# Linear attention and a gated feed-forward block: six tokens of r to a row, 384-token steps, a 32x32 convolution and a new order

## The chip, the cores and the metric

The kernel runs on one core of a Trainium2 chip. The metric is the device time of one execution in microseconds (us), as the median of several runs. A core has a tensor engine (PE, with its weight loads shown apart as PEld), a vector engine (DVE), a scalar engine (ACT), GpSimd (POOL) and a sync engine (SP), each with its own in-order queue of instructions, and 16 DMA engines that all queues share. PE writes to PSUM[...]; DVE and ACT read it.

## The reference

Two blocks in a row. The first is linear attention with a decaying state, for 4 batches, 8 heads, 768 tokens and 48 channels a head:

```python
for t in range(S):
    kt, vt, rt = k[:, :, t], v[:, :, t], r[:, :, t]
    cur = np.einsum('bhd,bhe->bhde', u[None] * kt, vt)
    y[:, :, t] = np.einsum('bhd,bhde->bhe', rt, state + cur)
    state = w[None, :, :, None] * state + np.einsum('bhd,bhe->bhde', kt, vt)
```

The second takes y, with the heads side by side, as x of 384 channels. It has a causal convolution of five taps for each channel, a sigmoid of it as a gate, and two 384x384 products:

```python
for j in range(5):
    gate_pre += conv_w[j] * xp[:, j:j + S, :]       # xp: x with four zero tokens ahead
out = (sigmoid(gate_pre) * (x @ w_val)) @ w_out
```

All inputs and the output are float32.

## The kernel before

**Tiling.** The tokens of a batch are cut into chunks of 128 (`C`), and two chunks make a unit (`W` = 256 tokens). Each batch has three units, so there are 12 units, numbered 0 to 11. The loop over time becomes, inside a chunk, a masked product of r and k (`attn`, `mask_at`) and, across chunks, a state that is carried (`state`, `carry`, `decay`). The powers of w are put into r and k beforehand by tables of exponentials (`dr`, `dk`, made by `decay_r` and `decay_k`).

**Loads.** `load_kv` (L69) brings one chunk of k or v with tokens on the partitions, so that each row is one token of one head, 192 bytes. `load_r` (L76) brings a unit of r with two neighbouring tokens on a partition, 384 bytes to a row. The scaled r is transposed on PE in two sets of 128 tokens, and the eviction `evac_r` (L282) puts the two sets back in order by writing with a stride of two. The weights `w_val` and `w_out` come in one transfer each.

**One unit, in stages.** Each stage has a token in the order: RS scales r (L260) and KS scales k (L289), mostly on POOL; RT and KT transpose them on PE (L274, L312), RE and KE evict them on ACT (L282, L322). PR multiplies the transposed k by r on DVE (L331), S sums it into the bonus of each token (L343), SE evicts that (L355), and DV multiplies v by it on POOL (L358). CV casts v to bfloat16 on ACT (L298). A is the product of k and r (L372), M its mask on DVE (L385). KV adds a chunk to the state (L399), ID adds the old state on DVE (L411), ZE multiplies it by the decay (L416). YD and Y collect y in PSUM (L427, L441), YE casts it to x, transposed, on ACT (L470).

**Feed-forward block.** It also works on units of 256 tokens. C is the convolution (L485): the five taps are diagonal 64x64 weights, and the products run on 64x64 tiles of the array. The 384 channels are three groups of 128; the third group is split over the two halves of the unit, so a unit needs two PSUM banks of 384 columns and 40 products. SG is the sigmoid on ACT (L498), V the product with `w_val` (L505, L514), HT its product with the gate on DVE (L527), O the product with `w_out` (L537), OE the eviction on ACT (L549), st the store (L553). The two chunks of the last unit go through smaller stages of their own (L575 to L652).

**The order.** The function emits each engine's instructions in the order of a long list of tokens, `ORDER`, that was found by a search; nothing reorders it afterwards. `RS:3` is the scaling of r for unit 3, `M:3.1` a mask of it, `k:3.0` a load; a star gives the stage to the other engine or queue. Since every engine works through its own part of this list in turn, the place of a token decides what it waits behind. Loads and stores stand in it too, nearly all on SP's queue; in before, all stores come after the last load. Waits between engines are put in from the data that the stages share. PSUM banks are handed out in turn (`bank`, eight buffers), and a buffer is taken again when its last reader is done.

Of the kernel before, what the change touches and what calls it, by code (L numbers as in the profile page):

```python
# [16 lines left out]
def kernel(  # L17
# [12 lines left out]
    nc = tc.nc  # L30
# [16 lines left out]
    ldr = ctx.enter_context(tc.tile_pool(name="ldr", bufs=6))  # L47
# [3 lines left out]
    outp = ctx.enter_context(tc.tile_pool(name="outp", bufs=11))  # L51
# [11 lines left out]
    def load_kv(n, cl, nm, eng):  # L63
        b, cu = divmod(n, NU)
        src, d = (k, k_st) if nm == "k" else (v, v_st)
        if n not in d:
            d[n] = ld.tile([128, U, H, D], F32, name=f"{nm}_st")
        t0 = cu * W + cl * C
        eng.dma_start(out=d[n][:, cl], in_=src[b, :, t0 : t0 + C, :].transpose([1, 0, 2]))  # L69

# [35 lines left out]
    io_i32 = consts.tile([128, 1], mybir.dt.int32)  # L106
    nc.gpsimd.iota(io_i32, pattern=[[0, 1]], base=0, channel_multiplier=1)
    io_j = consts.tile([128, 2], mybir.dt.int32)
    nc.gpsimd.iota(io_j, pattern=[[1, 2]], base=0, channel_multiplier=2)
    mask = consts.tile([128, 128], BF16)  # L110
    make_upper_triangular(nc, mask, val=1.0, diag=False)

    io_f = consts.tile([128, 1], F32)
    nc.vector.tensor_copy(io_f, io_i32)
    sc_k = consts.tile([128, U], F32)
    for cl in range(U):
        nc.vector.tensor_scalar(
            sc_k[:, cl : cl + 1], io_f, scalar1=-1.0, scalar2=float(C - 1 - cl * C),
            op0=ALU.mult, op1=ALU.add,
        )  # L120
    sc_r = consts.tile([128, 2], F32)
    nc.vector.tensor_copy(sc_r, io_j)
    nc.vector.tensor_scalar_add(sc_r, sc_r, float(-C))
# [4 lines left out]
    dr = consts.tile([128, H, 2, D], F32)  # L128

# [18 lines left out]
    def decay_r(x):  # L148
        for j in range(2):
            nc.scalar.activation(  # L150
                out=dr[:, halves(x), j, :],
                in_=lnw_bc[:, halves(x)],
                func=AF.Exp,
                scale=sc_r[:, j : j + 1],
            )

# [43 lines left out]
    nc.gpsimd.memset(wcm, 0.0)  # L200
    bdm = consts.tile([128, NP, 2, D], F32)
    nc.gpsimd.memset(bdm, 0.0)
    for par in range(2):
        nc.gpsimd.memset(bdm[64 * par : 64 * par + 64, :, par, :], 1.0)
# [3 lines left out]
    wv_st = consts.tile([128, NT, DM], F32)  # L208
    wo_st = consts.tile([128, NT, DM], F32)

    wval = consts.tile([128, NT, 4, 128], BF16)
    wout = consts.tile([128, 4, DM], BF16)
    cw5b = consts.tile([KW, DM], BF16)
    cwT = consts.tile([128, NT, KW], F32)
    cwd = consts.tile([128, NT, KW, 64], BF16)
    id64 = consts.tile([128, 64], BF16)

    for q in range(2):
        rows = slice(64 * q, 64 * q + 64)
        nc.vector.tensor_copy(id64[rows], ident[rows, rows])  # L220
# [11 lines left out]
    def cw_evac():  # L232
        nc.vector.tensor_copy(cwT, st["cw_ps"][:, :, 0:KW])

    def cw_diag():
        nc.vector.tensor_tensor(
            out=cwd.rearrange("p t k x -> p (t k) x"),
            in0=id64[:, None, :].to_broadcast([128, NT * KW, 64]),
            in1=cwT.rearrange("p t k -> p (t k)")[:, :, None].to_broadcast([128, NT * KW, 64]),
            op=ALU.mult,  # L240
        )

    def cast_wval():
        wv = wv_st.rearrange("p k (t x) -> p k t x", x=128)
        nc.gpsimd.tensor_copy(wval[:, :, 0::2, :], wv[:, :, 0::2, :])
        nc.gpsimd.tensor_copy(wval[:, :, 1::2, 64:128], wv[:, :, 1:3, 0:64])
        nc.gpsimd.tensor_copy(wval[:, :, 1::2, 0:64], wv[:, :, 1:3, 64:128])

    def cast_wout(part):
        if part:  # L250
            nc.scalar.copy(out=wout[64:128, 1::2, :], in_=wo_st[0:64, 1:3, :])
            nc.scalar.copy(out=wout[0:64, 1::2, :], in_=wo_st[64:128, 1:3, :])
        else:
            nc.gpsimd.tensor_copy(wout[:, 0::2, :], wo_st[:, 0::2, :])

    def scale_r(n, eng, ps=(0, NP)):
        hs = slice(2 * ps[0], 2 * ps[1])
        eng.tensor_tensor(  # L260
            out=rs_t[n % 2][:, :, ps[0] : ps[1], :, 0:D].rearrange("p s n a d -> p (n a) s d"),
            in0=r_st[n][:, hs],
            in1=dr[:, hs],
# [3 lines left out]
    def transp_r(n, ps=(0, NP)):  # L267
        if ("rT", n) not in st:
            st["rT", n] = wk.tile([128, NP, W], BF16, name="rT", bufs=3)
# [11 lines left out]
    def evac_r(n, ps=(0, NP)):  # L281
        nc.scalar.copy(  # L282
            out=st["rT", n][:, ps[0] : ps[1], :].rearrange("x n (i s) -> x s n i", s=2),
            in_=st["r_tr", n, ps[0]],
        )
# [10 lines left out]
    def cast_v(n):  # L296
        vb = vb_t[n % 4]
        nc.scalar.copy(  # L298
# [20 lines left out]
    def evac_k(n, cl=None):  # L319
        for cls, tr in st["tr", n]:  # L320
            if cl is None or cl == cls[0]:
                nc.scalar.copy(  # L322
                    out=st["kT", n].rearrange("x n (c i) -> x c n i", c=U)[:, cls[0] : cls[1]],
                    in_=tr,
# [84 lines left out]
    def carry(n, cl):  # L409
        kv_ps = st["kv_ps", n, cl]  # L410
        nc.vector.tensor_tensor(out=kv_ps, in0=kv_ps, in1=st["zin", n, cl], op=ALU.add)  # L411
# [55 lines left out]
    def evac_y(n, cl):  # L467
        b, cu = divmod(n, NU)
        t0 = PAD + cu * W + cl * C
        nc.scalar.copy(out=xT_t[b % 2][:, :, t0 : t0 + C], in_=st["y_ps", n, cl])  # L470


    def conv(n):
        b, cu = divmod(n, NU)
        xT, t0 = xT_t[b % 2], cu * W
        g_ps = [bank([128, W + C]) for i in range(2)]
        for T0, t1, tn in ((0, 0, W), (2, 0, 0)):
            for t in range(KW):
                for q in range(2):
                    for i in range(2):  # L480
                        T = 2 if T0 else i
                        c0, n0, o0 = (i * C, C, W) if T0 else (t1, tn, t1)
                        rows = slice(64 * q, 64 * q + 64)
                        qo = (q + i) % 2
                        nc.tensor.matmul(  # L485
                            out=g_ps[i][64 * qo : 64 * qo + 64, o0 : o0 + n0],
                            lhsT=cwd[rows, T, t, :],
                            rhs=xT[rows, T, t0 + c0 + t : t0 + c0 + t + n0],
                            start=(t == 0 and T0 == 0 and t1 == 0),
                            stop=(t == KW - 1),  # L490
                            skip_group_check=True,
                        )
        st["g_ps", n] = g_ps

    def gate_at(n, i):
        if ("gate", n) not in st:
            st["gate", n] = ffn.tile([128, 2, W + C], BF16, name="gate")
        nc.scalar.activation(out=st["gate", n][:, i], in_=st["g_ps", n][i], func=AF.Sigmoid)  # L498

    def value(n, i):  # L500
        b, cu = divmod(n, NU)
        xT, t0 = xT_t[b % 2], PAD + cu * W
        v_ps = bank()[:, 0 : W + C]
        for kt in range(NT):
            nc.tensor.matmul(  # L505
                out=v_ps[:, 0:W],
                lhsT=wval[:, kt, i, :],
                rhs=xT[:, kt, t0 : t0 + W],
                start=(kt == 0),
                stop=(kt == NT - 1),  # L510
                skip_group_check=True,
            )
        for kt in range(NT):
            nc.tensor.matmul(  # L514
                out=v_ps[:, W : W + C],
                lhsT=wval[:, kt, 2 + i, :],
                rhs=xT[:, kt, t0 + i * C : t0 + i * C + C],
                start=False,
                stop=(kt == NT - 1),
                skip_group_check=True,  # L520
            )
        st["v_ps", n, i] = v_ps

    def gated(n, i):
        if ("hT", n) not in st:
            st["hT", n] = ffn.tile([128, 2, W + C], BF16, name="hT")
        nc.vector.tensor_tensor(  # L527
            out=st["hT", n][:, i], in0=st["v_ps", n, i], in1=st["gate", n][:, i], op=ALU.mult
        )

    def project(n, cl):
        hT = st["hT", n]
        o_ps = bank()[:, 0:DM]
        parts = [(0, cl * C, 0), (1, cl * C, 1)]
        parts.insert(1 + cl, (cl, W, 2 + cl))
        for j, (i, c0, k) in enumerate(parts):
            nc.tensor.matmul(  # L537
                out=o_ps,
                lhsT=hT[:, i, c0 : c0 + C],
                rhs=wout[:, k, :],  # L540
                start=(j == 0),
                stop=(j == 2),
            )
        st["o_ps", n, cl] = o_ps

    def evac_o(n, cl):
        if ("o", n) not in st:
            st["o", n] = outp.tile([128, U, DM], F32, name="o_sb")
        nc.scalar.copy(out=st["o", n][:, cl, :], in_=st["o_ps", n, cl])  # L549

    def store(n):
        b, cu = divmod(n, NU)
        nc.sync.dma_start(  # L553
            out=out[b, cu * W : cu * W + W, :].rearrange("(c p) n -> p c n", p=128),
            in_=st["o", n],
        )

    HC = C // 2  # L560
    WL = C + HC

    def conv_l(n, cl):
        b, cu = divmod(n, NU)
        xT, t0 = xT_t[b % 2], cu * W + cl * C
        g_ps = [bank()[:, 0:WL] for i in range(2)]
        for T0 in (0, 2):
            for t in range(KW):
                for q in range(2):
# [262 lines left out]
```

## Time and profile before

| What | Value |
|---|---|
| Median of 3 runs | 103.78 us (103.75 to 104.38) |
| The profiled execution's own time | 103.68 us |
| Its span (first to last instruction) | 101.9 us |
| Granted PE clock, mean | 0.983 |
| Busy: PE, DVE, ACT, POOL | 84.5, 73.5, 72.7, 66.1 us |
| DMA packets, bytes | 67,505, 20.37 MB |
| Last product on PE ends (chain of waits) | 96.96 us |
| First store issued on SP | 75.90 us |

The profile is one execution seen by the hardware profiler. Its page gives busy time by engine, the span in 40 slices with a digit for the tenth of each slice that an engine was busy, the DMA queues, and groups of instructions. A group's row has its source line, engine and operation, what it writes and reads, the count, the busy time with the mean duration in nanoseconds, and the idle time ahead of it with what ended that idle time. The chain of waits follows the execution back from its end: each row is a start, a duration, and the work that held the end back at that time. A row of the waits has who waited, for whom, the sum in us, the times and the longest. A busy PE is one with at least one product in flight; several may overlap. Where many products follow each other, the time from the first of a stage to the first of the next is what the stage costs, and it is less than the count times the duration of one.

### The profile page before, as it was taken

Reading aid. Unit: us, or ns where it says so; the run is one execution under the profiler, and the core shown is the slowest. Engines: PE = TensorE matmul, PEld = TensorE weight load, DVE = VectorE, ACT = ScalarE, POOL = GpSimd, SP = SyncE. Lnnn points to the kernel's source line nnn. Section 1 sums busy time; section 2 is a strip of 40 time slices with the busy share of each in tenths; the row PEclk is TensorE's granted clock in tenths of the full one; section 3 lists DMA queues with packets and bytes.
Section 4 is the critical chain, followed back from the end, with each engine's and each line's share of the span. In section 5 each row is a group of like instructions: output and inputs, shape, how many; then the busy total and the mean of one; then the engine's idle time right before and its main releaser. Section 6 shows DMA issues by size and latency. Waiting matters only on the chain.

```text
span 101.9 us, 4626 instructions
## 1 busy us (share of the span) xinstructions
PE 84.5 (83%) x2017; PEld 69.4 (68%) x2017; DVE 73.5 (72%) x145; ACT 72.7 (71%) x126; POOL 66.1 (65%) x67
## 2 busy tenths in 40 slices
PE   1413987998969799989999999988999999999900
PEld 1202766876858587978887887876888788778500
DVE  4057798999765685889989998489678898980500
ACT  5457574999294998887988939688979868538510
POOL 7928678969499884999775686798692571400000
PEclk9999999999999999999999999999999999999985
DMA  0999999999989998999999999798989894750660
GB/s 7 253 220 168 234 175 192 270 244 171 277 165 249 203 216 180 200 185 250 173 191 223 187 248 222 142 204 187 185 162 251 306 363 145 271 198 7 250 218 5
DMA packets 67505, 20.37 MB, mean 200 GB/s; under 512 B 63510, under 2 KB 67484, under 8 KB 67484
## 3 DMA queue, kind: packets, MB, share of 16 engines
q1 hardware_dynamic: 64428, 19.18, 85.0%
q10 hardware_dynamic: 3056, 0.89, 4.0%
q8 instruction: 16, 0.26, 1.1%
q14 instruction: 5, 0.04, 0.1%
HBM read 15.35 MB, written 4.72 MB: 197 GB/s over the span
## 4 chain that ended last, share of the span: by engine, by line
PE 28%; SPq 24%; DMA 18%; POOL 12%; ACT 8%; issue 5%; POOLq 0%
SPq L69 19%; DMA v_st<-in_v_dram 15%; POOL dv L358 7%; PE bank L537 6%; PE bank L485 5%; PE bank L441 4%; POOL ks L289 4%; SPq L76 4%; DMA r_st<-in_r_dram 3%; ACT xT L470 2%; PE bank L505 2%; PE bank L427 2%; ACT kT L322 2%; PE bank L399 1%; ACT rT L282 1%
## 5 line engine op out<-in xcount | busy, mean ns | idle before, releaser
L385 DVE TENSOR_TENSOR at<-bank,mask 128x512 bf16<-128x512 f32 x48 | 30.9, 681 | 3.4 <-PE bank L372 3.3
L260 POOL TENSOR_TENSOR rs<-r_st,dr 128x768 bf16<-128x768 f32 x11 | 20.0, 1821 | 7.5 <-DMA r_st<-in_r_dram 7.5
L289 POOL TENSOR_TENSOR ks<-k_st,dk 128x768 bf16<-128x768 f32 x10 | 18.2, 1822 | 8.1 <-DMA k_st<-in_k_dram 4.4
L358 POOL TENSOR_TENSOR dv<-v_st,s_sb 128x768 bf16<-128x768 f32 x12 | 17.7, 1476 | 4.4 <-DVE s_sb L355 2.9
L282 ACT COPY rT<-bank 128x1024 bf16<-128x1024 bf16 (+1 forms) x13 | 15.9, 1231 | 2.6 <-PE bank L274 2.6
L322 ACT COPY kT<-bank 128x1024 bf16<-128x1024 bf16 (+1 forms) x13 | 12.5, 959 | 4.7 <-DVE pr L331 1.7
L527 DVE TENSOR_TENSOR hT<-bank,gate 128x384 bf16<-128x384 f32 x22 | 11.8, 552 | 4.2 <-PE bank L514 2.5
L470 ACT CAST xT<-bank 128x384 bf16<-128x384 f32 x24 | 11.0, 493 | 3.5 <-PE bank L441 3.5
L537 PE MATMUL bank<-wout,hT 128*128 128x384 bf16 x66 | 13.4, 327 | 0.0
L298 ACT CAST vb<-v_st 128x768 bf16<-128x768 f32 x12 | 10.0, 836 | 4.1 <-DMA v_st<-in_v_dram 4.1
L485 PE MATMUL bank<-xT,cwd 64*64 64x128 bf16 (+1 forms) x440 | 11.5, 245 | 0.9 <-ACT xT L470 0.4
L498 ACT ACTIVATE gate<-bank 128x384 bf16<-128x384 f32 x22 | 10.0, 493 | 2.6 <-PE bank L485 2.4
L485 PEld LDWEIGHTS <-cwd 64*64 64x64 bf16 x440 | 9.9, 106 | 2.5 <-issue 1.5
L549 ACT COPY o_sb<-bank 128x384 f32<-128x384 f32 x22 | 10.7, 501 | 1.2 <-PE bank L537 1.2
L505 PE MATMUL bank<-xT,wval 128*128 128x256 bf16 x66 | 10.8, 273 | 0.1
L312 PE MATMUL bank<-ident,ks 128*128 128x128 bf16 x96 | 8.8, 242 | 1.8 <-DVE ks L289 1.8
L372 PE MATMUL bank<-rT,kT 48*128 48x128 bf16 x192 | 9.0, 232 | 1.0 <-ACT kT L322 0.7
L331 DVE TENSOR_TENSOR pr<-bank,rT 128x1024 bf16<-128x1024 bf16 (+1 forms) x13 | 8.4, 645 | 1.9 <-ACT kT L322 1.3
L274 PE MATMUL bank<-ident,rs 128*128 128x128 bf16 x96 | 8.6, 242 | 1.1 <-DVE rs L260 0.8
L441 PE MATMUL bank<-at,vb 128*32 128x128 bf16 x384 | 9.0, 219 | 0.0
L312 PEld LDWEIGHTS <-ks 128*128 128x128 bf16 x96 | 6.8, 109 | 2.5 <-POOL rs L260 2.0
L274 PEld LDWEIGHTS <-rs 128*128 128x128 bf16 x96 | 6.7, 109 | 1.9 <-issue 1.0
(80 smaller groups left out, 137.8 us busy)
## 6 DMA issues: line engine op xcount, KB each, us to landing
k_st<-in_k_dram SPq DMA_DIRECT2D x24, 192.0 KB, 5.5
v_st<-in_v_dram SPq DMA_DIRECT2D x24, 192.0 KB, 4.5
out_dram<-o_sb SPq DMA_DIRECT2D x11, 384.0 KB, 4.5
r_st<-in_r_dram SPq DMA_DIRECT2D x9, 384.0 KB, 5.6
r_st<-in_r_dram ACTq DMA_DIRECT2D x2, 384.0 KB, 5.1
wv_st<-in_moe_w_val_dram SPq DMA_DIRECT2D x1, 576.0 KB, 6.2
wo_st<-in_moe_w_out_dram SPq DMA_DIRECT2D x1, 576.0 KB, 6.0
r_st<-in_r_dram SPq DMA_DIRECT2D x2, 192.0 KB, 3.5
```

The costliest lines, as they stand in the source:

```text
L69: eng.dma_start(out=d[n][:, cl], in_=src[b, :, t0 : t0 + C, :].transpose([1, 0, 2]))
L260: eng.tensor_tensor(out=rs_t[n % 2][:, :, ps[0] : ps[1], :, 0:D].rearrange("p s n a d -> p (n a) s d"), in0=r_st[n][:, hs], in1=dr[:, hs], ...
L274: nc.tensor.transpose(tr[:, s, p, :], rs_t[n % 2][:, s, ps[0] + p].rearrange("p a x -> p (a x)"), ident,)
L282: nc.scalar.copy(out=st["rT", n][:, ps[0] : ps[1], :].rearrange("x n (i s) -> x s n i", s=2), in_=st["r_tr", n, ps[0]],)
L289: eng.tensor_tensor(out=ks_t[n % 3][:, cs, :, :, 0:D].rearrange("p c n a d -> p c (n a) d"), in0=k_st[n][:, cs], in1=dk[:, cs], op=ALU.mult,)
L312: nc.tensor.transpose(tr[:, c, p, :], ks[:, cls[0] + c, p].rearrange("p a x -> p (a x)"), ident,)
L322: nc.scalar.copy(out=st["kT", n].rearrange("x n (c i) -> x c n i", c=U)[:, cls[0] : cls[1]], in_=tr,)
L358: eng.tensor_tensor(out=dv_t[n % 2].rearrange("p c (h d) -> p (c h) d", d=D), in0=v_st[n].rearrange("p c h d -> p (c h) d"), in1=st["s", n ...
L385: nc.vector.tensor_tensor(out=st["at", n, cl][:, par], in0=st["at_ps", n, cl][par], in1=mask[:, None, :].to_broadcast([128, NP, 128]), op= ...
L441: nc.tensor.matmul(out=y_ps[32 * q : 32 * q + 32, T, :], lhsT=lt, rhs=rh, start=False, stop=last, skip_group_check=True,)
L485: nc.tensor.matmul(out=g_ps[i][64 * qo : 64 * qo + 64, o0 : o0 + n0], lhsT=cwd[rows, T, t, :], rhs=xT[rows, T, t0 + c0 + t : t0 + c0 + t + ...
L537: nc.tensor.matmul(out=o_ps, lhsT=hT[:, i, c0 : c0 + C], rhs=wout[:, k, :], start=(j == 0), stop=(j == 2),)
```

## The change

Seven things are done together.

1. **r.** Batch 0 keeps its loads by unit. For batches 1 to 3, `load_rb` brings four heads of a whole batch at a time with six neighbouring tokens on a partition, 1,152 bytes to a row. A table `drb` of six exponentials of 128x384 is added (`decay_rb`, on ACT). "Unit" q of such a batch is now the token set {6p + 2q, 6p + 2q + 1}; `evac_r` writes into a transposed tile of the whole batch with a stride of six, so attention of the batch can begin when all three sets are there.
2. **Feed-forward steps.** They are 384 tokens, two a batch, and 384, 256 and 128 for the last batch: nine steps. The special stages for the last unit go.
3. **Convolution.** The taps are diagonal 32x32 weights, and a step has 5 x 3 x 4 = 60 products on 32x32 tiles, three PSUM banks a step. The channels of each group come out turned by a multiple of 32; the columns of `w_val` and the rows of `w_out` are turned to fit, the latter by five loads in place of one.
4. **Stores.** An output row of a partition is three neighbouring tokens, 4,608 bytes. The last product therefore reads `hT` with a stride of three. The staging buffers of the two weights are now two of the six buffers of the output ring.
5. **State.** The old state is added on PE by a product with the identity instead of on DVE.
6. **Engines.** Some evictions may go to DVE, some casts of v and the cast of `w_out` to POOL: four KE, six YE and four OE go to DVE, two CV to POOL; two RS and one KS more go to DVE. Some set-up moves between POOL and DVE.
7. **Order.** The whole list is new, searched with at most one engine reading a PSUM bank at a time. It has four groups of dummy products (three of 512 columns each, `D`) and places the store of step 2 ahead of the last load.

The core of the diff, with the old list left out:

```diff
-    ldr = ctx.enter_context(tc.tile_pool(name="ldr", bufs=6))
+    ldr = ctx.enter_context(tc.tile_pool(name="ldr", bufs=3))
...
-    outp = ctx.enter_context(tc.tile_pool(name="outp", bufs=11))
+    outp = ctx.enter_context(tc.tile_pool(name="outp", bufs=6))
...
+    G = 2 * NU
+
+    def load_rb(b, eng, x):
+        if ("rb", b) not in r_st:
+            r_st["rb", b] = ldr.tile([128, H, G, D], F32, name="rb_st", bufs=2)
+        hs = slice(H // 2 * x, H // 2 * x + H // 2)
+        eng.dma_start(
+            out=r_st["rb", b][:, hs].rearrange("p h s d -> p h (s d)"),
+            in_=r[b, hs].rearrange("h (p s) d -> p h (s d)", s=G),
+        )
...
+    def decay_rb(j):
+        nc.scalar.activation(out=drb[:, :, j, :], in_=lnw_bc, func=AF.Exp, scale=sg[:, j : j + 1])
...
+    wv_st = outp.tile([128, NT, DM], F32, name="o_sb")
+    wo_st = outp.tile([128, NT, DM], F32, name="o_sb")
+
+    wval = consts.tile([128, NT, NT, 128], BF16)
+    wout = consts.tile([128, NT, DM], BF16)
...
+    def load_wout(i):
+        T, (c0, f0, n0) = [(T, x) for T in range(NT) for x in turned(T)][i]
+        nc.sync.dma_start(
+            out=wo_st[c0 : c0 + n0, T, :], in_=moe_w_out[128 * T + f0 : 128 * T + f0 + n0, :]
+        )
+
+    def cast_wout(pool):
+        if pool:
+            nc.gpsimd.tensor_copy(wout, wo_st)
         else:
-            nc.gpsimd.tensor_copy(wout[:, 0::2, :], wo_st[:, 0::2, :])
-
-
+            nc.scalar.copy(out=wout, in_=wo_st)
...
+            in0=r_st["rb", b][:, hs, two] if b else r_st[n][:, hs],
+            in1=drb[:, hs, two] if b else dr[:, hs],
...
+            dst = st["rTb", b].rearrange("x n (i s) -> x s n i", s=G)[:, 2 * q : 2 * q + 2]
...
-        kv_ps = st["kv_ps", n, cl]
-        nc.vector.tensor_tensor(out=kv_ps, in0=kv_ps, in1=st["zin", n, cl], op=ALU.add)
+        nc.tensor.matmul(
+            out=st["kv_ps", n, cl].rearrange("p n a d -> p (n a d)"),
+            lhsT=ident,
+            rhs=st["zin", n, cl].rearrange("p n a d -> p (n a d)"),
+            start=False,
+            stop=True,
+            skip_group_check=True,
+        )
...
+    def taps(g_ps, xT, t0, n0):
+        for t in range(KW):
+            for T in range(NT):
+                for b in range(4):
+                    rows, q = slice(32 * b, 32 * b + 32), 32 * ((b + T) % 4)
+                    nc.tensor.matmul(
+                        out=g_ps[T][q : q + 32, 0:n0],
+                        lhsT=cwd[rows, T, t, :],
+                        rhs=xT[rows, T, t0 + t : t0 + t + n0],
+                        start=(t == 0),
+                        stop=(t == KW - 1),
+                        skip_group_check=True,
+                    )
+
+    STEPS = [(b, f, 3) for b in range(B - 1) for f in (0, 3)]
+    STEPS += [(B - 1, 0, 3), (B - 1, 3, 2), (B - 1, 5, 1)]
...
+                lhsT=st["hT", m][:, T, 0 : span(m)[2]].rearrange("p (i c) -> p c i", i=C)[:, j],
+                rhs=wout[:, T, c0 : c0 + n0],
+                start=(T == 0),
+                stop=(T == NT - 1),
...
     ORDER = """
+        w r:1* wt:1 r:0.0 WB:0 LN:0 k:0.0 r:0.1 WB:1 wt:0 DRI:0 LN:1 DRI:1 k:1.1 RSP:0.0 RTP:0.0
+        k:1.0 ut:1 RSP:0.1 D:8 DKI:0 k:0.1 cw r:2* RTP:0.1 RS:1 k:2.0 RT:1 DKI:1 KS:1* DRB:1 CWB
+        Wo:1 REP:0.1 RS:2 KSP:0.1 ut:0 k:2.1 KT:1 v:0.1 KTP:0.1 KSP:0.0 RE:1 v:0.0 UW KTP:0.0 Wo:3
+        rb:1.1* KE:1* KEP:0.0 KS:2 A:1.0 KEP:0.1 REP:0.0 PR:1 rb:1.0 DRB:5 M:1.1 Wo:2 DRB:3 v:1.1
+        A:1.1 v:1.0* PR:0 A:0.1 S:1 k:3.1 k:4.0 WCT M:0.3 M:1.3 WCM S:0 CWT SE:1 RT:2 DRB:4 A:0.0
+        SE:0 CV:0 M:1.0 Wo:0 Wv KV:0.0 DV:0 DRB:0 M:1.2 RS:3 KT:2 M:0.1 RE:2 M:0.2 D:14 ZE:0.0
+        M:0.0 YD:0 DRB:2 TL Y:0.1 KE:2* k:3.0 CV:1 Y:0.0 DV:1 YE:0.0 RS:4* CWD PR:2 KV:0.1 RT:3
+        ZE:0.1 v:2.1 A:2.0 YD:1 RT:4 YE:0.1* Y:1.0 S:2 v:2.0 Wo:4 RS:5 v:3.0 RE:3 KV:1.0 YE:1.0*
+        RE:4 ID:1.0 ZE:1.0 v:3.1 C:0 SE:2 Y:1.1 M:2.0 RT:5 M:2.1 KS:3* SG:0.2 A:2.1 KV:1.1 SG:0.1
+        WV YE:1.1 RE:5 DV:2 ZE:1.1 k:4.1 V:0.2 k:5.0 M:2.3 KT:3 V:0.1 CV:2 HT:0.2 V:0.0 k:5.1
+        M:2.2 KV:2.0 rb:2.1 HT:0.1 YD:2 ID:2.0 Y:2.0 ZE:2.0 KE:3 SG:0.0 YE:2.0 HT:0.0 WO* CV:3
+        PR:3 A:3.0 M:3.1 A:3.1 Y:2.1 O:0.1 YE:2.1 KS:4 S:3 KV:3.0 V:1.1 OE:0.1 M:3.0 C:1 SE:3 KT:4
+        ZE:3.0 KV:3.1 M:3.3 DV:3 V:1.0 SG:1.0 SG:1.2 v:4.0 v:4.1 M:3.2 O:0.2 YD:3 PR:4 SG:1.1
+        rb:2.0 V:1.2 v:5.1 ZE:3.1 HT:1.1 HT:1.0 KS:5 S:4 KE:4 Y:3.0 A:4.0 k:6.0 SE:4 A:4.1 YE:3.0
+        Y:3.1 v:5.0 HT:1.2 CV:4 KT:5 O:1.0 M:4.1 OE:0.2* M:4.3 KV:4.0 k:6.1 OE:1.0 O:1.1 k:8.1
+        ID:4.0 M:4.0 rb:3.0 DV:4 M:4.2 YD:4 KE:5 RS:6 O:0.0 ZE:4.0 k:8.0 Y:4.0 OE:1.1 OE:0.0 k:7.1
+        k:7.0 Y:4.1 YE:4.0 YE:4.1 PR:5 KV:4.1 rb:3.1 S:5 A:5.1 ZE:4.1 A:5.0 RT:6 YE:3.1 SE:5 M:5.2
+        CV:5 C:2 M:5.3 V:2.2 RE:6 v:6.0 SG:2.2 RS:7 RS:8* KS:6 RT:7 M:5.0 HT:2.2 KV:5.0 SG:2.0
+        RE:7 DV:5 KS:8 M:5.1 RT:8 v:6.1 v:7.1 v:7.0 KT:6 ID:5.0 V:2.1 YD:5 ZE:5.0 KE:6* V:2.0
+        k:9.0 RE:8 Y:5.0 v:9.1 Y:5.1 A:6.0 SG:2.1 PR:6 v:9.0 v:8.1 HT:2.1 HT:2.0 A:6.1 KS:7 O:1.2
+        YE:5.1* O:2.1 M:6.3 O:2.0 S:6 OE:1.2 YE:5.0 M:6.0 KT:7 KT:8 OE:2.0 OE:2.1 k:9.1 M:6.1
+        M:6.2 SE:6 PR:8 V:3.1 C:3 S:8 KE:7 V:3.0 RS:9 PR:7 CV:6 SG:3.1 k:10.0 KE:8* SG:3.2 HT:3.1
+        DV:6 KV:6.0 RT:9 SG:3.0 ZE:6.0 O:2.2 S:7 KV:6.1 SE:8 HT:3.0 OE:2.2 SE:7 YD:6 v:8.0 CV:7
+        V:3.2 ZE:6.1 HT:3.2 RE:9 RS:10 v:10.1 RS:11 A:7.1 A:7.0 Y:6.0 Y:6.1 KV:7.0 RT:10 M:7.3
+        M:7.2 k:10.1 YE:6.1 YE:6.0 ID:7.0 v:10.0 O:3.2 M:7.1 M:7.0 RE:10 ZE:7.0 DV:7 A:8.1 M:8.2
+        RT:11 k:11.0 O:3.1 YD:7 KS:9 M:8.3 KV:7.1 Y:7.0 RE:11 Y:7.1 YE:7.0 OE:3.2* A:8.0 M:8.1 C:4
+        OE:3.1 CV:9 M:8.0 CV:8* YE:7.1 ZE:7.1 KT:9 V:4.2 KV:8.0 V:4.0 DV:8 KS:10 V:4.1 SG:4.2 PR:9
+        HT:4.2 k:11.1 ID:8.0 KV:9.0 SG:4.0 HT:4.0 KE:9 SG:4.1 YD:8 A:9.0 v:11.0 ZE:8.0 A:9.1
+        ZE:9.0 Y:8.1 M:9.1 Y:8.0 YE:8.1 HT:4.1 KT:10 M:9.2 KV:9.1 st:2 O:4.0 CV:10* YE:8.0 KE:10
+        OE:4.0 C:5 M:9.0 O:4.2 M:9.3 ZE:9.1 SG:5.1 SG:5.0 PR:10 SG:5.2 v:11.1 S:9 KS:11 A:10.0
+        M:10.1 A:10.1 KT:11 O:4.1 SE:9 KV:10.0 OE:4.2 M:10.0 M:10.3 S:10 DV:9 ID:10.0 KE:11 OE:4.1
+        SE:10 O:3.0 V:5.0 ZE:10.0 V:5.2 OE:3.0 DV:10 PR:11 KV:10.1 M:10.2 V:5.1 HT:5.0 S:11
+        ZE:10.1 SE:11 YD:10 st:4 YD:9 Y:10.0 CV:11 Y:9.0 Y:9.1 HT:5.2 HT:5.1 YE:10.0 DV:11 Y:10.1
+        YE:9.0 YE:9.1* A:11.0 A:11.1 YE:10.1 C:6 M:11.2 SG:6.1 M:11.3 KV:11.0 V:6.2 st:3 M:11.0
+        SG:6.0 ID:11.0 M:11.1 V:6.1 YD:11 ZE:11.0 V:6.0 Y:11.0 Y:11.1 HT:6.1 SG:6.2 YE:11.0* O:5.2
+        YE:11.1* C:7 HT:6.2 O:5.0 O:5.1 st:0 HT:6.0 V:7.0 OE:5.2 OE:5.1 O:6.0 SG:7.2 OE:5.0*
+        SG:7.0 O:6.1 O:6.2 V:7.2 OE:6.1 V:7.1 OE:6.0* OE:6.2 V:8.0 HT:7.0 C:8 SG:7.1 st:1 st:5
+        HT:7.2 V:8.2 HT:7.1 SG:8.2 O:7.1 O:7.0 SG:8.1 SG:8.0 HT:8.0 st:6 V:8.1 HT:8.2 OE:7.1
+        HT:8.1 Oa:8 Ob:8 Xb:8 OE:7.0 st:7 D:22 Xa:8 sta:8 D:25 stb:8
```

## The prediction

> **What bounds the kernel now.** I read the page's busy row, slices and DMA rows first, then the chain of waits in order of time, the groups by form and the waits.
>
> ```profile
> PE 84.5 (83%) x2017; PEld 69.4 (68%) x2017; DVE 73.5 (72%) x145; ACT 72.7 (71%) x126; POOL 66.1 (65%) x67
> ...
> PE   1413987998969799989999999988999999999900
> ...
> DMA  0999999999989998999999999798989894750660
> ...
> DMA packets 67505, 20.37 MB, mean 200 GB/s; under 512 B 63510, under 2 KB 67484, under 8 KB 67484
> ...
> q1 hardware_dynamic: 64428, 19.18, 85.0%
> q10 hardware_dynamic: 3056, 0.89, 4.0%
> ```
>
> The DMA engines are full from the first microseconds to about 75 us, PE from about 35 us to 97 us: two limits that overlap. Nearly all packets are small. The chain joins the two:
>
> ```profile
> 35.14 1.02 PE bank L485 x40
> 36.17 0.55 PE bank L274 x8
> 36.72 0.49 PE bank L537 x3
> 37.21 0.17 PE bank L399 x4
> 37.38 0.45 PE bank L312 x8
> 37.82 0.33 PE bank L505 x3
> 38.15 0.17 PE bank L514 x3
> ...
> 60.89 5.63 DMA v_st<-in_v_dram
> 66.52 0.03 POOLq L358
> 66.55 0.12 POOL rs L260
> 66.67 1.00 issue
> 67.67 1.49 POOL dv L358
> ```
>
> Up to 69 us it runs through loads and POOL, after that through PE alone. The PE rows are prices of whole stages in a dense stretch. POOL, which scales what is loaded, chases the loads (the waits):
>
> ```profile
> POOL rs L260 <- DMA r_st<-in_r_dram: 7.5, 9, 2.1
> POOL ks L289 <- DMA k_st<-in_k_dram: 4.4, 4, 3.0
> ```
>
> **PE's work and its idle time.** Prices from chain and timeline: r or k transposes 0.46 us, attention 0.28 a chunk, state 0.17, bonus 0.18, y from the bonus 0.34, y 0.50, convolution 1.02 a unit, value 0.50 a half, projection 0.49 per 128 tokens. Over the order of before that is 75.8 us. PE's last product ends at 96.96, so 21.2 us are idle or stretched. I call "idle" at a stage its start less the PE work ordered ahead of it: 15.4 at 21.2 us, 17.3 at the y of unit 2 (30.55), 19.9 at the k transposes of unit 7 (54.54), 21.2 at the end. Span 101.9 is PE's end plus 4.9 (last eviction, store, end); the execution took 103.68, 1.8 more than its span, and the median of the runs is 103.78.
>
> [...] (200 GB/s with 192 and 384 B rows, 357 GB/s at 80 to 85 us, where only 1,536 B rows move). [...] 40 convolution products of 192 columns on average took 1.02 us, 25.5 ns each; alone, a product of 384 columns takes 163 ns (0.49 for three), so 192 take 82 ns and four side by side would allow 20 ns. [...] in before the k eviction (L322) does wait 1.7 us for the product pr that reads the same bank, so one reader at a time is nothing new on that bank.
>
> **The change part by part.**
>
> *DMA.* Both queues' packets took (85.0% + 4.0%) x 101.9 = 90.7 us of 16 engines. At 80 to 85 us 1,536 B packets took 1.01 x 5 x 16 us for 1.79 MB: 70 ns each. With 3,072 packets of 192 B, 768 of 384 B and 240 of 1,536 B per engine, a fixed part plus a part per byte gives 10.3 ns + 0.0389 ns/B: 17.8 ns (192 B), 25.2 (384 B), 55 (1,152 B), 189 (4,608 B). r of batches 1 to 3: 576 x 25.2 = 14.5 us becomes 192 x 55 = 10.6: 3.9 us less. Stores: 192 rows x 70 = 13.4 becomes some 10.8 us, but they lie behind the loads. The 1,152 B price is interpolated, 45 to 65 ns: 2 to 6 us saved. Adding up what each load has ahead of it, k of unit 7 goes from 48.7 to 51.6 us of DMA time (its order was moved back, and r of batch 3 comes before it), the last k from 76.1 to 70.9, and the last v from 77.2 to 74.7 with one store (1.5) slipped ahead. SP keeps its loads back to back: of the stores only step 2's stands ahead of a load, and its outputs are made long before. The output ring shrinks to six buffers, two of them first the weights', so the evictions of step 6 wait until the store of step 0 has landed. That store follows the one of step 3, whose last projection has 57 us of PE work ahead: issued near 79 us, landed near 84; step 6 is projected with 70 us ahead, near 90. Without these 6 us, ACT would hold the gates of steps 7 and 8 behind that eviction, and PE would wait for them. ACT's queue gets four large loads instead of two, 0.4 us of issue each (L76 on ACT).
>
> *Convolution.* 11 x 1.02 + 1.0 = 12.2 us goes. A step of 384 tokens has 60 products on 32x32 tiles, 12 of them distinct. 163/12 = 13.6 ns if all 12 overlap; before reaches 1.25 times its bound (25.5 against 20), so I take 17 ns: 1.02 us a step, 8.2 us for the eight steps' worth. Gain 4.0 us. From below 13.6 ns (6.5 us in all); from above 25.5 ns, the pace of before (12.2), and 163/4 = 41 ns if only row groups overlap (19.6).
>
> *Value and projection.* Nine products of 384 columns a step, 1.47 us, against 1.50 for as many tokens: 0.3 less in all. Projection keeps its three products; its weights hT are read with a stride of three elements, which no row shows. A contiguous load takes 97 ns under a 163 ns product; I take 0, and above 163 ns the excess would come through 72 times.
>
> *Carry on PE.* Eight products of 384 columns: +1.3 us on PE, -4.5 on DVE (L411, 8 x 564 ns). *Dummies:* four times three products of 512 columns, 0.64 us each; two early (+1.3 counted), two after the last projection, under the 4.9 us tail.
> PE in all: 75.8 - 4.0 - 0.3 + 1.3 + 1.3 = 74.0 us up to the last projection.
>
> *DVE.* Off: carry 4.5, the diagonal build halves (1.75 to 0.9), small casts 1. On: four k evictions (nearest row pr, 128x1024 with two inputs, 0.69; 0.5 to 1.1) 2.7, six y and four output evictions at 0.55 (L416's shape) 5.0, two r scalings at 1.0, one k scaling 1.0, memsets 1. Sum 73.5 + 5.3 = 78.8 us. *ACT.* Off: 4 x 1.03, 6 x 0.49, 4 x 0.50, two casts of v 1.7, weight casts 1.7; on: six exponentials 128x384 at 0.61 = 3.7. 72.7 - 8.6 = 64. The r eviction now writes with a stride of 6 elements; stride 2 cost 1.33 us against 1.03 contiguous; I take 1.33, from 1.03 to 2.0, hidden in ACT's 36 us of slack; without it, nine times 0.7. *POOL.* Three scalings less (5.4), two casts of v, one weight cast of 1,152 elements (1.2) and five weight pieces for three: about 63. Each of these has room; what hides them is PE.
>
> **Where the end comes from.** k of unit 7 has 51.6 us of DMA ahead; in before the same load was used 2.6 us after its sum (48.7, scaling at 51.25). So scaling ends at 51.6 + 2.6 + 1.8 = 56.0. Ahead of its transposes the new order has 35.9 us of PE work (idle 20.1), behind it 38.1. PE ends at 94.1 at best. From unit 7's transposes to the end before added 1.3 us of idle; the same gives 95.4, span 95.4 + 4.9 = 100.3, time 100.3 + 1.8 = 102.1. Other loads bind less: unit 11's last k is scaled at 75.3 with 56 ahead (idle 19.3). What is late next is DVE's work for units 9 and 10.
>
> **Rivals.** *The saved time is spent early* (no change). r of batch 1 comes whole ahead of v of unit 1 and of w_val. w_val lands at 26.2 + 2.6, its casts take 2.7 (1.75 + 0.50 + 0.50), so the first value starts at 31.5 with 12.5 us ahead: idle 19.0, where before had 17.3 at that time. If PE then adds 3.9 us as before did, it ends at 74.0 + 22.9 = 96.9: 103.6. For it: full DMA slices in that stage. Against: later loads come sooner.
> *The small tiles do not overlap twelve-fold* (slower). Nothing in before runs more than four tiles. At 25.5 ns the convolution costs 4.0 us more than I count: PE ends near 99.4, time 106.1. It decides from 21 ns on, where PE's work is the 75.8 of before again. Against: y's 28 products with four column tiles come at 14 to 18 ns.
> *DVE becomes the bound* (slower). At 40 to 60 us it is busy 18.3 of 20; 1.07 times as much is 19.6. If half of the added 5.3 us shows, 104.7.
>
> **How the numbers follow.** Likeliest case 0.56 (own range 99.2 to 103.5: convolution at 13.6 ns saves 1.6, no friction 1.3 on one side; landing 4.0 us after the sum, as for the last k of before, on the other), spent early 0.17, tiles 0.13, DVE 0.14. About 1% is what a measurement of this kernel can tell from no change; the likeliest case gives 0.48 faster and 0.08 within, spent early all within, the other two slower: 0.48, 0.25, 0.27. The range runs from 99.0 to 106.0.
>
> **What would show it.** 60 products at about 1.0 us a step; last k scaled near 75 us, last load landed by 78; PE's idle near 20 at unit 7's transposes; DVE under 80 us and PE still dense after 56 us. I am wrong if a step of the convolution takes over 1.25 us, if PE's gaps after 56 us are ended by DVE, or if the loads end no earlier than 79 us.

## The result and the profile after

The changed kernel takes 124.69 us (median of 4 runs, 123.14 to 126.45), beside 104.08 us for the kernel before on the same chip (4 runs): a ratio of 1.188, 95% interval 1.175 to 1.201. It was forecast at 102.1 us. The profiled execution took 124.23 us, with a span of 122.5. Medians here are of all runs, while a ratio leaves out those that the chip ran in a slower state, so a ratio can differ a little from the quotient of the medians.

The page of the changed kernel, with the rows shown of before (busy time, slices, packets and queues):

```profile
PE 94.4 (77%) x1979; PEld 66.6 (54%) x1979; DVE 79.6 (65%) x154; ACT 86.2 (70%) x115; POOL 61.1 (50%) x70
...
PE   2389279916496899997735999589399999959993
...
PEclk9999965798559999999995599977859999999999
DMA  3999999997969999789899970900000008910455
...
DMA packets 59392, 20.36 MB, mean 166 GB/s; under 512 B 54246, under 2 KB 58348, under 8 KB 59372
...
q1 hardware_dynamic: 54748, 18.40, 62.8%
q10 hardware_dynamic: 4624, 1.67, 6.1%
```

DMA did what it was meant to do: with the second queue's 6.1% its packets took 68.9% of 122.5 = 84.4 us of 16 engines, against 90.7 before, and hardly anything moves from 80 to 101 us (slices 27 to 33): the loads no longer set the end. But PE has holes, also where it was dense before (slices 9 to 13, 19 to 22, 26 and 29), and its granted clock falls in them or just after. Of the three busy times that were forecast one is far off: ACT, 86.2 us where 64 were expected. The chain of waits and the waits on POOL, of which the prediction showed the rows of before, read now:

```profile
88.25 1.82 PE bank L514 x46
...
96.18 1.20 PE bank L514 x60
...
119.24 1.29 PE bank L177 x6
```

```profile
POOL dv L382 <- DVE s_sb L379: 15.0, 4, 6.6
POOL ks L314 <- PE bank L423: 9.6, 3, 4.3
```

The chain holds PE almost alone and begins at 88 us, so it doesn't show what went on before. POOL's longest waits are no longer for the loads but for DVE and PE, which are late themselves. The row of groups with the largest excess is the eviction of r (columns: busy time, mean ns of one, idle time before it); the lines after it are from the view of its output tile, which lists who waited for it and how long (us, times):

```profile
L310 ACT COPY rTb<-bank 128x1024 bf16<-128x1024 bf16 x9 | 32.1, 3657 | 1.1 <-PE bank L297 1.1
```

```profile
DVE pr L355: 5.0, 1
PE bank L297: 4.7, 2
DVE at L409: 3.8, 4
PE bank L547: 3.6, 2
```

Each of the nine takes 3.66 us, and PE is among those that wait for it. The timeline of the first stretch shows how. ACT first, then PE (start, duration, instruction, and in brackets the idle time ahead with what ended it):

```profile
25.14 3.59 ACT L310 COPY rTb<-bank 128x1024 bf16<-128x1024 bf16 x1
29.42 3.60 ACT L310 COPY rTb<-bank 128x1024 bf16<-128x1024 bf16 x1 [0.69 <-PE bank L297]
34.94 0.87 ACT L539 ACTIVATE gate<-bank 128x384 bf16<-128x384 f32 x2 [1.92 <-PE bank L514]
```

```profile
28.78 0.61 PE L297 MATMUL bank<-ident,rs 128*128 128x128 bf16 x8 [2.66 <-ACT rTb L310]
...
33.07 1.80 PE L514 MATMUL bank<-xT,cwd 32*32 32x384 bf16 x56 [1.78 <-ACT rTb L310]
...
40.40 0.65 PE L547 MATMUL bank<-xT,wval 128*128 128x384 bf16 x3 [1.67 <-ACT rTb L310]
```

Each of the three begins 0.05 us after an eviction ends (28.73, 33.02 and 40.35 us). PE wants a PSUM bank that the eviction hasn't given back, and everything behind that instruction in PE's fixed order stands still. The last two aren't about r at all: a convolution and a value product of the feed-forward step read nothing that the eviction writes. What they can share with it is a bank, whose turn has come while ACT is still reading it.

**PE's idle time by stage.** Counted as in the prediction (a stage's start less the PE work ordered ahead of it, good to some 0.3 us), with two of the experiments below beside it:

| Stage | Changed kernel | r in runs of 32 | Pairs, made late |
|---|---|---|---|
| r transposes of unit 3 | 16.0 | 17.2 | 16.5 |
| y from the bonus, unit 2 (after the evictions of units 3 to 5) | 26.4 | 18.3 | 24.0 |
| r transposes of unit 6 | 27.2 | 18.9 | 26.0 |
| k transposes of unit 7 (after those of 6 to 8) | 35.2 | 19.6 | 34.5 |
| r transposes of unit 11 (after 9 and 10) | 38.0 | 19.8 | 35.5 |
| k transposes of unit 9 (after all nine) | 42.0 | 19.8 | 42.0 |
| projection of step 5 | 43.7 | 21.1 | 45.0 |

The lost time comes in three portions, one for each batch, and hardly any of it after the ninth eviction. Between the first two columns it grows by 22.6 us at the end. The nine evictions differ by 9 x (3.66 - 1.02) = 23.8 us: nearly all of it comes through.

### The profile page after: what moved, and what is told of

Read it like the earlier page. It is cut to its first block, busy times and chain, and to the rows that moved or that the text cites. A ratio compares the mean times of both kernels' runs of the same rounds, so it can differ in the third digit from the quotient of the medians.

```text
span 122.5 us, 4550 instructions
## 1 busy us (share of the span) xinstructions
PE 94.4 (77%) x1979; PEld 66.6 (54%) x1979; DVE 79.6 (65%) x154; ACT 86.2 (70%) x115; POOL 61.1 (50%) x70
## 3 DMA queue, kind: packets, MB, share of 16 engines
HBM read 15.35 MB, written 4.72 MB: 164 GB/s over the span
## 5 line engine op out<-in xcount | busy, mean ns | idle before, releaser
L310 ACT COPY rTb<-bank 128x1024 bf16<-128x1024 bf16 x9 | 32.1, 3657 | 1.1 <-PE bank L297 1.1
L547 PE MATMUL bank<-xT,wval 128*128 128x384 bf16 (+2 forms) x81 | 15.7, 311 | 3.6 <-ACT rTb L310 3.6
L571 PE MATMUL bank<-wout,hT 128*128 128x384 bf16 (+1 forms) x75 | 17.1, 357 | 0.3 <-DVE hT L559 0.3
L539 ACT ACTIVATE gate<-bank 128x384 bf16<-128x384 f32 (+2 forms) x27 | 11.2, 472 | 6.0 <-PE bank L514 4.7
L559 DVE TENSOR_TENSOR hT<-bank,gate 128x384 bf16<-128x384 f32 (+2 forms) x27 | 13.3, 507 | 2.7 <-ACT gate L539 1.6
L514 PE MATMUL bank<-xT,cwd 32*32 32x384 bf16 (+2 forms) x540 | 11.1, 349 | 3.8 <-ACT xT L501 2.0
L278 POOL TENSOR_TENSOR rs<-rb_st,drb 128x768 bf16<-128x768 f32 x7 | 12.7, 1821 | 1.1 <-DMA rb_st<-in_r_dram 0.7
L514 PEld LDWEIGHTS <-cwd 32*32 32x32 bf16 x540 | 6.9, 94 | 7.3 <-issue 5.7
L547 PEld LDWEIGHTS <-wval 128*128 128x128 bf16 x81 | 7.1, 99 | 6.8 <-issue 4.3
L571 PEld LDWEIGHTS <-hT 128*128 128x128 bf16 x75 | 7.2, 109 | 4.5 <-issue 1.8
```

The lines of the kernel that those rows point to most:

```text
L278: eng.tensor_tensor(out=rs_t[n % 2][:, :, ps[0] : ps[1], :, 0:D].rearrange("p s n a d -> p (n a) s d"), in0=r_st["rb", b][:, hs, two] if b ...
L310: nc.scalar.copy(out=dst, in_=st["r_tr", n, ps[0]])
L514: nc.tensor.matmul(out=g_ps[T][q : q + 32, 0:n0], lhsT=cwd[rows, T, t, :], rhs=xT[rows, T, t0 + t : t0 + t + n0], start=(t == 0), stop=(t ...
L547: nc.tensor.matmul(out=v_ps, lhsT=wval[:, kt, T, :], rhs=xT_t[b % 2][:, kt, PAD + t0 : PAD + t0 + n0], start=(kt == 0), stop=(kt == NT - 1),)
L559: nc.vector.tensor_tensor(out=st["hT", m][:, T, 0:n0], in0=st["v_ps", m, T], in1=st["gate", m][:, T, 0:n0], op=ALU.mult,)
L571: nc.tensor.matmul(out=o_ps, lhsT=st["hT", m][:, T, 0 : span(m)[2]].rearrange("p (i c) -> p c i", i=C)[:, j], rhs=wout[:, T, c0 : c0 + n0] ...
```

## The experiments

Theory 1: the eviction of r, written with a step of six elements, is the whole loss. Rivals: the lowered clock of PE is a cause of its own (theory 2); the new order or another part is at fault (theory 3); the wide writes hinder the other engines beyond the time that ACT spends on them (theory 4).

**The same eviction, written in runs.** Undoes the step alone. It leaves out the ordering of r's tokens, so attention of batches 1 to 3 works on permuted r and the output isn't the reference's. The core of the edit:

```diff
-  dst = st["rTb", b].rearrange("x n (i s) -> x s n i", s=G)[:, 2 * q : 2 * q + 2]
+  dst = st["rTb", b].rearrange("x n (u g j) -> x g (n u) j", g=G, j=32)
+  dst = dst[:, 2 * q : 2 * q + 2]
+  src = src.rearrange("x s n (u j) -> x s (n u) j", j=32)
```

> The changed kernel, with one edit: ScalarE's eviction of r for batches 1 to 3 writes 32 neighbouring elements at a time instead of every sixth element. Same tile, same instruction count, same waits; the tokens of r inside a batch are not put back into order, so attention of batches 1 to 3 works on permuted r. If the six-element step is the cause (theory 1), the nine evictions fall from 3.66 us to 1.0 to 1.3 us, ScalarE's busy time from 86 to 62 to 66 us, TensorE is granted its full clock in nearly every slice, and the time is 100 to 105 us. If TensorE's lowered clock is a cause by itself (theory 2), the evictions shorten but the slices of 0.6 to 0.8 stay, and the time is 110 us or more. If the new order or another part is the cause (theory 3), the evictions shorten, the clock returns, and the time is still 110 us or more, with TensorE waiting for something else than these evictions between 30 and 45 us.

It took 102.24 us (101.57 to 103.78), beside 105.09 for before in the same session: 0.974, interval 0.968 to 0.980. From its page, the busy row and the granted clock, then the group of the eviction:

```profile
PE 86.8 (87%) x1979; PEld 63.1 (63%) x1979; DVE 77.6 (78%) x154; ACT 63.9 (64%) x115; POOL 61.3 (61%) x70
...
PEclk9999999999999999999999999999999999999999
...
L313 ACT COPY rTb<-bank 128x1024 bf16<-128x1024 bf16 x9 | 9.2, 1018 | 1.7 <-PE bank L297 1.5
```

And from the timeline of PE, the same six products early and a little later:

```profile
22.31 0.85 PE L460 MATMUL bank<-ident,dv 128*128 128x128 bf16 x6
...
25.66 0.51 PE L460 MATMUL bank<-ident,dv 128*128 128x128 bf16 x6
```

With this one edit the rest of the prediction's sum comes true: ACT 63.9 us (64 forecast), unit 7's k transposes at 55.35 us, right after their scaling (forecast to end at 56.0), span 99.8 (100.3), time 102.24 (102.1). Theories 2 and 3 fall.

The clock needs care. The row shows nines from the start, but the trace has no record of the clock before 24.9 us, and until then products are slow: the six above take 0.85 us, later 0.51. Before, the changed kernel and the pairs below start in the same way, with slow products until 20.0, 23.0 and some 23.6 us, so these early microseconds don't tell the kernels apart (in the mean of 0.983 given for before, the time up to 20.0 us, of which there is no record, counts as full; what is missing lies after 98.5 us, behind PE's last product). After 25 us the clock stays full to the end of PE's work here, in before and with the pairs below, where no gap in PE's work is longer than 1.5 us. In the changed kernel, after its own slow start, it is halved four times, from 29.8, 64.0, 81.0 and 87.9 us on, for 20.5 us in all, each time within about a microsecond of the end of a gap of 2.0 to 2.7 us. The one edit takes away both these gaps and the halved clock, so here the clock is a consequence of the nine evictions and no cause of its own.

**The same eviction, in pairs.** Each element lands where it does in the changed kernel; ACT only goes through them in another order.

```diff
-  dst = st["rTb", b].rearrange("x n (i s) -> x s n i", s=G)[:, 2 * q : 2 * q + 2]
+  dst = st["rTb", b].rearrange("x n (i s) -> x n i s", s=G)[:, :, :, 2 * q : 2 * q + 2]
+  src = src.rearrange("x s n i -> x n i s")
```

> The changed kernel, with one edit: the same eviction goes through its elements so that two neighbouring tokens are written one after the other (4 bytes, then a jump of 12), and the step is taken on the reading side, in PSUM. If the price is set by each separate place that is written (theory 1a), the eviction falls from 3.66 us to about 1.9 to 2.2 us and the time to 104 to 110 us. If it is set by each 2-byte element whatever its neighbour is (theory 1b), it stays at 3.3 us or more and the time at 120 to 125 us. Theories 2 and 3 expect 118 us or more either way.

> The pairwise eviction once more, unchanged, in more rounds: it computes all that the reference asks for and is the candidate that could beat both kernels. Theory 1 with the sum of the prediction expects 101.5 to 104.5 us, a ratio to before of 0.975 to 0.995. If TensorE's lowered clock near 20 us, seen in its first profile, belongs to this kernel and wasn't chance, it stays at 104 to 105.5 us, not to be told from before.

```profile
L312 ACT COPY rTb<-bank 128x1024 bf16<-128x1024 bf16 x9 | 9.5, 1056 | 1.8 <-PE bank L297 1.7
```

The eviction took 1.06 us, not the 1.9 to 2.2 or 3.3 that the two readings allowed: two neighbours of 2 bytes written one after the other cost next to nothing more than a contiguous row (1.01 us in the price list below). The time was 104.19 us (102.36 to 104.90, 4 runs; before 105.09), and in the longer comparison 103.54 (100.94 to 105.52, 6 runs; before 105.21), a ratio of 0.981 with an interval of 0.957 to 1.006. The fault is mended at no cost, but this kernel can't be told from before with certainty. The low clock near 20 us in the first profile (a mean of 0.67 from 10 to 20 us and of 0.82 from 20 to 30) is a slow start like that of the other kernels. It doesn't explain the time: the three shortest of the ten runs (100.94, 101.89 and 102.36 us) have a mean clock of 0.95 to 0.97, the seven others 0.95 to 1.00. By the order, PE falls behind the kernel with runs of 32 between 33 and 52 us, to 21.8 us of idle time at the k transposes of unit 6 against 19.4, in both profiles, and by little more after that. Why, isn't settled.

**r loaded by unit again.** Two tokens to a row, a tile of its own for each unit, written with a step of two, no row scales for six tokens (DRB), and seven buffers for the loads in place of three; all the other parts of the change stay. The loads in the order, in short:

```diff
-  rb:1.1*   rb:1.0    rb:2.1  rb:2.0    rb:3.0  rb:3.1
+  r:3*      r:4 r:5   r:6     r:7 r:8   r:9     r:10 r:11
```

> The changed kernel with the loads of r undone alone: r of batches 1 to 3 comes by unit of 256 tokens, two tokens to a row, and is written with a step of two; no copy of it is taken on GpSimd. The 384-token steps, the 32x32 convolution and the new order stay. Theory 1: evictions at 1.33 us, ScalarE at 63 to 67 us, the clock back, 102 to 107 us (the loads of r cost the queue about 3.9 us more than in the changed kernel, and come later than its order was made for). Theories 2 and 3: 112 us or more.

105.92 us (104.79 to 106.78; before 105.09), nothing like 124. The clock came back but for 3.4 us (a mean of 0.83 from 50 to 60 us, 1.00 in every other stretch of 10 us after 30), after a gap of 2.0 us near 51 us. Beside before it shows that the 384-token steps, the small convolution tiles and the new order together gain nothing that can be seen, in an order that was searched for the six-token rows; one searched for rows of two was not tried. Beside the two kernels above, the six-token rows bring some 2 to 4 us in this order, once the eviction is cheap.

**Two price lists.** They compute nothing of the reference: copies of 128 x 1,024 elements, three of each form.

> A price list and no part of the reference's work: copies of 128 x 1,024 bfloat16 elements from PSUM to SBUF on ScalarE and on VectorE, three of each form, with the output in steps of one, two, three, four, six and eight elements, in runs of 2, 4, 8 and 16 neighbours at a three-fold pitch, and as the pairs of the experiment before; and 12 matrix multiplies with the weights read at a step of one and of three elements. Theory 1 expects ScalarE at about 1.03 us for one, 1.33 for two and 3.6 for six. If each write pays for the place it opens, the price is the same from three or four on, and runs of 4 or more are back near 1.0 to 1.3 us. If it pays for distance, it grows from four to six to eight in proportion. VectorE: 0.6 us for one; if the write side of SBUF is what is slow, its price at six is also near 3.6 us, and if it is ScalarE's own, VectorE stays at 0.6 to 1.1 us. Weights at a step of three cost what weights at one do, within 20 ns.

The groups of the first list (mean ns of one is the second number after the bar):

```profile
L47 ACT COPY act_step_eight<-srcbf 128x1024 bf16<-128x1024 bf16 x3 | 14.3, 4755 | 0.1
...
L47 ACT COPY act_step_six<-srcbf 128x1024 bf16<-128x1024 bf16 x3 | 10.8, 3585 | 0.1
L45 DVE COPY dve_step_six<-srcbf 128x1024 bf16<-128x1024 bf16 x3 | 10.7, 3562 | 0.1
...
L47 ACT COPY act_step_two<-srcbf 128x1024 bf16<-128x1024 bf16 x3 | 3.9, 1294 | 0.1
...
L47 ACT COPY act_run_two_of_three<-srcbf 128x1024 bf16<-128x1024 bf16 x3 | 3.1, 1031 | 0.1
...
L47 ACT COPY act_step_one<-srcbf 128x1024 bf16<-128x1024 bf16 x3 | 3.0, 1012 | 6.7 <-PE srcbf L40 6.6
```

On ACT, steps of one, two, three, four, six and eight cost 1.01, 1.29, 1.86, 2.44, 3.59 and 4.76 us. From two on that is a straight line, 0.56 to 0.59 us for each further element of step. Step one lies above it: the line would have 0.72 there. DVE follows the same line (1.29 to 4.72 us), and its 0.69 for step one lies near it. Runs of two, four, eight or sixteen neighbours at three times the pitch cost 1.01 to 1.03 us on ACT (DVE 0.82 for two, 0.69 from four on). The prices don't level off from three or four elements on, as one of the readings had it. The stride-three weights gave no excess (326 ns for a product on average, 493 for contiguous ones, which ran first, in an execution with a mean clock of 0.547), so the comparison isn't clean.

> A second price list, no part of the reference's work: what decides the price of a wide step. 1,024 float32 at steps of one, two, four and six (4 to 24 bytes), pairs of bfloat16 at pitches of 8, 16 and 24 bytes, on ScalarE and VectorE; single bfloat16 at a step of six with an SBUF source in place of PSUM, and the reading side at a step of six with a contiguous output, on ScalarE, VectorE and GpSimd. If the distance in bytes sets it and the pairs were cheap because there are half as many places, 512 pairs at 24 bytes cost about half of 1,024 single elements at 24 bytes, so well over 2 us, and float32 at 24 bytes about 7 us. If 2-byte writes alone are slow and 4 bytes pass at full rate, pairs stay near 1.03 us at every pitch, and float32 is near 1.0 to 1.6 us. A source in SBUF changes nothing (3.5 us); reading at six is cheaper than writing at six.

```profile
L49 ACT COPY sbuf_to_six<-sb 128x1024 bf16<-128x1024 bf16 x3 | 10.8, 3610 | 0.0
...
L49 ACT CAST float_six<-srcbf 128x1024 f32<-128x1024 bf16 x3 | 6.0, 2001 | 0.1
...
L51 DVE COPY sbuf_to_six<-sb 128x1024 bf16<-128x1024 bf16 x3 | 5.6, 1882 | 8.4 <-ACT sbuf_to_six L49 8.4
...
L49 ACT COPY act_pair_of_six<-srcbf 128x1024 bf16<-128x1024 bf16 x3 | 3.1, 1049 | 0.1
```

Distance alone isn't it: pairs of 2-byte elements cost 1.03, 1.06 and 1.05 us on ACT at pitches of 8, 16 and 24 bytes (DVE 0.69, 1.05 and 1.05). Single float32 elements cost 1.08 and 1.15 us at 4 and 8 bytes and 2.00 at both 16 and 24, which neither reading foresaw. The source doesn't matter to ACT (3.61 us out of SBUF); DVE out of SBUF writes a step of six in 1.88 us, which wasn't expected either. GpSimd takes 3.61 us. Reading with a step of six out of SBUF and writing a row costs 1.57 us on ACT.

**The cost alone, in the kernel before.** A second copy of the bank, step four, ahead of each of the nine evictions; its output is read by nobody.

```diff
+  if n >= 3:
+      nc.scalar.copy(
+          out=late.rearrange("x (i s) -> x s i", s=4)[:, 0],
+          in_=st["r_tr", n, ps[0]].rearrange("x s n i -> x (s n i)"),
+      )
```

> The kernel before, with the suspected cost alone: ahead of each of the nine evictions of r of batches 1 to 3, ScalarE copies the same PSUM bank once more, into a tile nobody reads, with an output step of four (2.43 us in the price list). Bank and r come free that much later; loads, orders, steps and diagonal are those of before. If nine evictions of some 3.7 us are enough to explain the loss whatever the order (theory 1), ScalarE's busy time rises from 72.7 to about 94 us and the time to 112 to 126 us, TensorE again waiting for PSUM banks. If the loss needs the new order or the new steps as well (theory 3), it is 104 to 108 us.

```profile
L285 ACT COPY late<-bank 128x1024 bf16<-128x1024 bf16 x9 | 22.6, 2507 | 3.7 <-PE bank L274 3.7
```

119.42 us (117.92 to 120.42; before 105.21): 1.151, interval 1.128 to 1.173. The extra copies took 9 x 2.51 = 22.6 us, ACT was busy 92.8 us, and the time rose by 14.2 between the medians. Before's order hides more of it, but a late eviction of r alone is enough to lose at least two thirds of what was lost. The mean clock of the profiled execution was 0.967 over a span of 116.1 us, 3.8 us short of full. So the clock can account for some 3.8 us at most (an estimate from these two figures), and most of the 14.2 us is waiting.

**The cost alone, in the changed kernel with pairs.** The pairwise copy is done two and a half times more ahead of the last one. The core of the edit:

```diff
+  for m in (NP, NP, NP // 2):
+      nc.scalar.copy(out=dst[:, 0:m], in_=src[:, 0:m])
```

> The changed kernel with the pairwise eviction (1.06 us), made late again without any wide step: ScalarE does the same pairwise copy two and a half times more ahead of the last one, some 3.7 us in all for each of the nine. Nothing writes single elements at a step of six. If it is ScalarE's time that costs (theory 1), it is back at 118 to 128 us, with TensorE's clock lowered in the stretches where it waits. If the single elements do harm beyond ScalarE's own time, by holding up the other engines' accesses to SBUF (theory 4), it stays clearly below the changed kernel, at 104 to 115 us.

124.72 us (123.83 to 125.59), 1.207 of before, interval 1.186 to 1.228: the changed kernel's time. The groups are the extra copies and the last one:

```profile
L311 ACT COPY rTb<-bank 128x1024 bf16<-128x1024 bf16 x18 | 19.0, 1055 | 0.3
...
L314 ACT COPY rTb<-bank 128x1024 bf16<-128x1024 bf16 x9 | 9.3, 1039 | 0.3
```

With nine half copies of 0.60 us that is 33.7 us for the nine evictions, against 32.1, and none of them writes single elements at a step of six. It is ACT's time and its place in the order that cost; theory 4 falls.

## Why the prediction was wrong

**The step that failed** is in the part on ACT: "The r eviction now writes with a stride of 6 elements; stride 2 cost 1.33 us against 1.03 contiguous; I take 1.33, from 1.03 to 2.0, hidden in ACT's 36 us of slack; without it, nine times 0.7". Two things in it were wrong.

First the size: 3.66 us measured, outside the range that was given. Step one and step two were taken as two points of a price that had nearly levelled off. The price list has step two as the first point of a line that goes on rising; 1.33 us in proportion to the step would have given 4.0 us. A step of four already costs 2.44 us there.

Second the cover. "36 us of slack" is the span less ACT's busy time. It says nothing on when ACT must be done, and the eviction sits where that counts: it holds a PSUM bank that PE's fixed order will ask for a few instructions on, and r itself is wanted next. The excess was 9 x (3.66 - 1.33) = 21.0 us and the time was missed by 22.6. The sentence's own fallback, the excess with the cover gone, was the right sum with the wrong price, and no rival was made of it.

**Right, as the experiment with runs of 32 shows.** The load sum (unit 7's k scaled by 55.3 us, 56.0 forecast), PE's idle time there (20.1 forecast, 19.6) and at the end (21.4, 21.1), ACT at 64 us, the span. The kernel with pairs, which computes what the reference asks for, has 21.7 us of idle time there and 103.5 to 104.2 us, inside the range. In the changed kernel itself: a convolution of 384 columns 0.97 to 1.20 us where the clock is full (1.02 forecast; 1.82 where it is halved), three projection products 0.49 us with stride-three weights, DVE's k eviction 0.68 (0.69), its y and output evictions 0.55, DVE 79.6 us (78.8), POOL 61.1 (63).

**Other sizes that were off, without weight.** r scalings on DVE 1.88 us (1.0 forecast), and the weight cast on POOL 1.87 (1.2), though 1.14 in the kernel with runs. Two readings in the prediction are wrong by little. Before's k transposes of unit 7 start at 53.70 us and not at 54.54, so the idle time there was some 19.1 us, 2.1 were added behind it and not 1.3, and the same sum gives 102.9 us. Ten evictions at 0.55 us make 5.5 on DVE and not 5.0.

**The rivals.** The small tiles overlap as was hoped (60 products in 0.97 to 1.20 us, 16 to 20 ns each). DVE isn't the bound: it is idle for 43 of 122.5 us. "Spent early" isn't what lost the time, though the early stretch did cost what that rival said: in the kernel with runs the first value starts at 30.83 us with some 18.5 idle (31.5 and 19.0 forecast), and about 3 us follow where it feared 3.9. The likeliest case was right in its mechanism for a kernel whose eviction is cheap, and the case that decided was missing: an engine with slack made late at one place.

**The signs that were named.** "PE still dense after 56 us" failed, as it should have; but most of the gaps were ended by ACT, which the list of what would prove the forecast wrong didn't have. One item of the list did come true: the last load landed at about 79.4 us ("no earlier than 79"), since SP stood from 70.6 to 75.9 us at the store of step 2, whose outputs it took to be "made long before". That is a consequence: by 71 us PE was already 15.6 us behind the kernel with runs.

**Open.** Why single 2-byte writes pay by distance and pairs don't; what part of the 22.6 us is PE's halved clock and what is waiting (20.5 us at half the clock can cost at most 10.2, an estimate; PE's busy time is 7.6 us above that of the kernel with runs); and whether the kernel with pairs beats before by 1 to 2%.

## What to carry to other kernels

When an access pattern changes, give the new pattern a price of its own or bound it by proportion, and look at how many elements are written side by side: let the innermost loop write at least two neighbouring elements and put the step on the side that reads (1.06 us here, against 3.66). Four bytes alone are not enough: single float32 elements at 16 bytes cost 2.00 us, pairs of bfloat16 1.06. Busy share is no cover: for each instruction that grows, name what it holds (a bank, a buffer) and which in-order engine asks for that next. An excess on such an instruction can come through almost whole, times its count: 22.6 of 23.8 us here, 14.2 of 22.6 in before's order.

## What the hardware did that was not expected

- Single bfloat16 elements written from PSUM at a step cost 0.56 to 0.59 us more for each further element of step from two on (1,024 a partition), on ACT and DVE alike, up to 4.76 us at eight; pairs at 24 bytes cost 1.05 us.
- float32 at 16 and 24 bytes costs the same, 2.00 us, about half of a 2-byte element at 12 bytes (3.59).
- DVE writes a step of six in 1.88 us from SBUF and 3.56 from PSUM; ACT takes 3.6 from either.
- PE's clock was halved for 3.4 or 6.8 us at a time in the changed kernel, near the end of gaps of 2.0 to 2.7 us in its work; in 10 us windows that lowers the mean to 0.67 to 0.72 (30 to 40, 60 to 70, 80 to 90 us), where a kernel that differs in one access pattern stayed at 1.0. Gaps of 1.3 to 1.7 us in the same execution were not followed by it. From what length of a gap on it falls was not measured.
